# State products of three batch pairs kept in DRAM, w_in in its own column order, the score operand loaded in one piece of 128 rows, and a new hand-written order

## The chip, the cores and the metric

One core of one Trainium2 chip runs the whole program. The metric is device microseconds of one execution. All values in and out are float32; the matmul operands are rounded pieces of float32 ("hi" and "lo"), so that three matmuls (hi·hi, hi·lo, lo·hi) stand for one product.

## What is computed

`x` is [8, 8, 512, 64] (batch, heads, tokens, depth), `state` is [8, 8, 32, 64]. Each head attends both ways, and the 512 token reads and 32 state reads of a batch are then rows of a feed-forward layer:

```python
scores = scale * x @ state.T          # softmax over the 32 states -> a
xread  = a @ state
scores2 = scale * state @ x.T         # softmax over the 512 tokens -> a2
sread  = a2 @ x
rows = concat([xread, sread])         # 8 * 544 = 4352 rows of 512
h = rows @ w_in                       # 512 x 1024
solu = h * softmax(h)
ln = (solu - mean) / sqrt(var + 1e-6) * g_ln
out = ln @ w_out                      # 1024 x 512
```

`w_in` and `w_out` come as 64-bit floats and are turned into float32 on the chip from their two 32-bit words.

## The kernel before, in words

**Fold.** `xread @ w_in` is `a @ (state @ w_in)`. For each pair of batches k (0 to 3) the products state·w_in are made first (`state_w_in`, step V{k}{c}{n}: row block c of w_in, column half n; three matmuls into one PSUM bank at line 277, then two copies of 64 rows each, line 282, into the tiles `swf` of the two batches). `split_state_w_in` (step P) rounds `swf` to `swh` and keeps the rest as `swl`. The 32 token tiles of 128 rows (t = 0 to 31, four per batch) then multiply the softmax matrix with these (`h_steps`, step H, line 447: 12 matmuls). The two last tiles, t = 32 and 33, hold the state reads of all batches and multiply with `whi`/`wlo` themselves.

**A batch.** `load_x` (steps LT) brings the transposed x as two tiles `xT` of 128 partitions, each by two loads of 64 partitions (line 170); `load_xn` (Ln) brings x by tokens; `score` (S, line 319) makes all scores in two PSUM banks; `softmax_tokens` (E) and `softmax_states` (A) make both softmaxes, E with a round trip through DRAM (`e2d`); `read_tokens` (R, line 400) makes the state reads.

**A tile.** After H the chain C (lines 454 to 477: maximum, exponential, product, centring, square sum, scale); then the bounce D (lines 483 to 488: a transpose of 32x32 blocks on VectorE, a store `ut` to DRAM and a load `back` that rearranges it); then T (lines 491 to 502: `uh` and `ul`, rounded part and rest); then O (line 514: 24 matmuls with `wohi`, `wolo`), a scaled copy `osb` and a store: line 527 for token tiles, lines 530 and 531 for the tiles of state reads. There the DRAM side is `b r d` with four batches outermost, while the SBUF side has 128 rows.

**Weights.** `load_w` (l0 to l7 w_in, l8 to l15 w_out, 512 KB each), `low_words` (cl, ScalarE, line 193), `to_f32` (c, VectorE and GpSimd, lines 204 to 210), `split_w_in` (wi: `whi` on ScalarE, `wlo` on VectorE, both written through `placed`, line 216, a strided view that puts the 1024 columns in the order in which the bounce wants them), `split_w_out` (wo: `wohi`, `wolo`, with -g folded in).

**Order.** `ORDER` is a list written out in the file; `issue` walks it and takes one yield of the named step at each word (`*n`: n of them). Every engine has one queue, worked strictly in that order; all loads and stores are issued by SyncE (SP), and a step that waits holds up whatever follows on its engine. `OPT` gives, by letters (a ScalarE, d VectorE, p GpSimd), the engine of each copy, subtraction and so on. The step K is a matmul of the identity with itself, put where TensorE would be idle. The tiles share 43 blocks of 4 KB a partition (`k4`). PSUM has four banks for `ps_t` and four for two h tiles.

The order before begins:

```
K l0 Lg l1 l2 l3 l4 l5 LT000 LT001 LT010 c0 cl0 l6 c0 l7 l8 c0 l9 cl1 c1 l10 c1 l11 LT011 c1 Ls0 cl2 Ls1 Lg c2 l12
wi0 c2 l13 l14 c3 l15 c2 c3 Ln00 cl3 Ln01 Ln10 cl4 Ln11 wi0 c3 cl5 c4 wi1 c4 c5 c4 c5 wi1 c5 cl6 c6 wi2 c6 c7*2 cl7
wi2 cl8 c7 c8 cl9 c8*2 c9 wo0 c10*2 cl10 c9 c10 Q0 G0 c9 cl11 c6 wo1 c11 K*60 S0 LT100 LT101 LT110 LT111 G1 c11 wi3
wo1 A0 c11 cl12 A0 wo2 A0 Q0 wo3 Q1 wi3 K*14 V000 Ls2 A0 cl13 cl14 c12 V000 V001 c12 V000 Q1 V001 A0 V010 wo0 Ls3
c12 V010 A0 V001 cl15 V011 A0 wo4 V010 A0 E0 V011 V020 wo4 P00 E0 A0 V011 P00 E0 V021 wo2 A0 V030*2 E0 H0 A0 H0
V030 V021 H1 V020 wo3 V031 V021 H1 V031 c13 V100 E0 Q2 c14 H0 V031 E0 H1 c14 V101 V020 Q2 c14 V110 P01 V101 V111
V100 P10 H0 c15 H1 c15 P01 P11 E0*2 V101 H0 c15 V100 V110 E0 H0 V111 c13 H1 P20 H1 P11 C0 V110 S1 LT200 LT201 C1
V111 E0 C0 G2 E1 C1 C0 E1 c13 C1 H2 C0 H2 R0 C0 D0 R0 Ln20 Ln21 H3 wo5 C0 R0 D0 H3 A1 E1 R0 wo5 H3 wo6 R0 H3 E1 H3
```

Of the kernel before, what the change touches and what calls it, by code (L numbers as in the profile page):

```python
# [8 lines left out]
F32 = mybir.dt.float32  # L9
# [9 lines left out]
P = 128  # L19
# [9 lines left out]
OPT = dict(ph=2, k4=43, nat=[], s2='p', add='ddpdppdddddppppp', whi='aaaa', wlo='dddd', spl='ppdp',  # L29
           ev='aadaadaaaadaaaaddadadaaaaaadddddaaaaaadadaaaaaadaddadaaaadaadada', swh='aaaaaaaddaddddad',  # L30
           swl='pppppdpppppppdpd', sub='pppppppp', mul='ppdddppd', ath='adaddada', alo='ppdppppd',
           up='aaadadaaadadadaaadaddddaadadaadaaa',
           uh='adaaaddaaadadaddaaadddadddaadaadaddadaddaaaadadaaaaaaaadadaadddaaaad',
           ul='dpdpppppddppppppddpddpdpdpppddpppdppdppppdppppddddddpdpppddpppppdddd',
           oe='aaddaaddaadadadaddadaaddaaaadddaaa')

ORDER = """
K l0 Lg l1 l2 l3 l4 l5 LT000 LT001 LT010 c0 cl0 l6 c0 l7 l8 c0 l9 cl1 c1 l10 c1 l11 LT011 c1 Ls0 cl2 Ls1 Lg c2 l12
wi0 c2 l13 l14 c3 l15 c2 c3 Ln00 cl3 Ln01 Ln10 cl4 Ln11 wi0 c3 cl5 c4 wi1 c4 c5 c4 c5 wi1 c5 cl6 c6 wi2 c6 c7*2 cl7
wi2 cl8 c7 c8 cl9 c8*2 c9 wo0 c10*2 cl10 c9 c10 Q0 G0 c9 cl11 c6 wo1 c11 K*60 S0 LT100 LT101 LT110 LT111 G1 c11 wi3  # L40
wo1 A0 c11 cl12 A0 wo2 A0 Q0 wo3 Q1 wi3 K*14 V000 Ls2 A0 cl13 cl14 c12 V000 V001 c12 V000 Q1 V001 A0 V010 wo0 Ls3
c12 V010 A0 V001 cl15 V011 A0 wo4 V010 A0 E0 V011 V020 wo4 P00 E0 A0 V011 P00 E0 V021 wo2 A0 V030*2 E0 H0 A0 H0
# [15 lines left out]
D10 C11 O8*2 T8 D11 V221 O8 C11 O8 T8 O8 V221 T8 O8 T9 O8*2 T9 T10 O8 T10 O8*3 D11 T10 T9 T10 O9 T9 O8 O9*2 O8 O9*4
T11 O9*2 T11 O9 T11 O9 T11 O9 H13 O9 H13*2 O9 H13 V230 R2 V230 V231 R3 R2 V230 R2 R3 H12 V231 R3*2 S4 P40 P41 V231
C12 O10*3 E4 C12 O10 C13 E4 O10*2 C12 O10 C13 O10*2 C12 H14 C13 H14*2 C12 C13 H14*2 D12 C13 H14 C12 H15 D13 D12 H15  # L60
E4 H15 C13 H15 E4 D13 H15 LT500 P50 LT501 H15 E4*2 P41 LT510 O10 A4 LT511 O10 D12 A4 O10 A4 O11 D13 O11*2 P50 E4*2
O11*3 O10 E4 O11 P51 S5 LT600 LT601 A4 O10 C14 O11*2 E5 O11 LT610 LT611 C14 O11 P51 T12 O11 T12 A4 O12*3 T12 T13
# [40 lines left out]
def attention_then_solu_ffn(ctx, tc, xT, xn, stB, w_in, w_out, g, out):  # L103
# [515 lines left out]
```

## Time and profile before

| what | us |
|---|---|
| median of 3 runs (417.55 to 417.89) | 417.82 |
| profiled execution: its own time | 420.33 |
| its span, first to last instruction | 418.6 |
| PE busy in the span | 369.9 |
| VectorE (DVE) busy | 332.9 |
| ScalarE (ACT) busy | 221.6 |
| GpSimd (POOL) busy | 198.5 |

The transfers that SP issues move 79.18 MB and take 59.6% of 16 DMA engines' span.

How to read it: busy time counts the instructions of an engine, not its waits. PE's is the union of overlapping, pipelined matmuls, so that the mean duration of a matmul in a row (about 0.39 us for 512 columns) is more than the distance from one to the next. The groups of instructions give mean durations by line and tile name; the DMA view gives transfers with the median from issue to landing; the stretches of time give each engine's busy time, the DMA engines' busy share (mean over 16, 1.00 is all of them) and GB/s between two times. Times in all of them are microseconds from the span's start.

### The profile page before, as it was taken

How to read it: one execution, taken by the hardware profiler on the slowest of the kernel's cores; microseconds unless marked ns; L12 is line 12 of the kernel's file. 1: busy time of each engine (PE TensorE's matmuls, PEld its weight loads, DVE VectorE, ACT ScalarE, POOL GpSimd, SP SyncE). 2: the span in 40 equal slices, each digit the busy share in tenths (PEclk: the TensorE clock that was granted, in tenths of full speed). 3: DMA queues.
4: the chain of work that ended last, by engine and by line, in shares of the span. 5: the costliest groups of instructions: out<-in, count | busy, mean ns of one | idle time of the engine just before them, and what ended most of it. 6: DMA issues, size and time to landing. Idle time of an engine off the chain costs nothing.

```text
span 418.6 us, 6204 instructions
## 1 busy us (share of the span) xinstructions
PE 369.9 (88%) x2222; PEld 285.6 (68%) x2222; DVE 332.9 (80%) x436; ACT 221.6 (53%) x347; POOL 198.5 (47%) x257
## 2 busy tenths in 40 slices
PE   8606593887999989999989999989999999999995
PEld 8603362665876768886667676768768688788875
DVE  2898999898998998848989898886899957653631
ACT  2647686666536644827257364534537636624631
POOL 0206787586741746234864448636553214423300
PEclk9955799799999989999999999999999999999998
DMA  7999804776377586950898848545214385352361
GB/s 221 229 313 365 172 8 133 246 225 227 109 249 221 178 276 201 302 176 27 223 294 283 297 161 224 188 148 194 108 69 144 109 290 203 115 198 82 145 201 50
DMA packets 43194, 79.57 MB, mean 190 GB/s; under 512 B 3100, under 2 KB 24860, under 8 KB 43164
## 3 DMA queue, kind: packets, MB, share of 16 engines
q1 hardware_dynamic: 43164, 79.18, 59.6%
q8 instruction: 17, 0.28, 0.3%
q14 instruction: 13, 0.11, 0.1%
HBM read 48.24 MB, written 30.93 MB: 189 GB/s over the span
## 4 chain that ended last, share of the span: by engine, by line
PE 32%; DVE 30%; DMA 23%; issue 6%; ACT 4%; POOL 3%; SPq 2%; DVEq 0%; POOLq 0%; ACTq 0%
PE o L514 17%; PE h L447 11%; DMA back<-ut 7%; DMA ut<-ub 6%; DMA xT<-xT_dram 5%; DVE u L460 4%; DVE ub L483 3%; DVE sm L454 3%; DMA st<-stB_dram 3%; DVE wolo L236 2%; DVE wf L207 2%; DVE z L368 2%; PE swps L277 2%; DVE swf L134 2%; DVE ul L137 2%
## 5 line engine op out<-in xcount | busy, mean ns | idle before, releaser
L137 POOL TENSOR_TENSOR ul<-back,uh 128x512 fp32r<-128x512 f32 x40 | 54.5, 1366 | 59.4 <-DVE uh L134 34.7
L514 PE MATMUL o<-wohi,uh 128*128 128x512 f32 (+1 forms) x280 | 76.4, 394 | 6.8 <-DVE uh L134 3.1
L514 PE MATMUL o<-wolo,uh 128*128 128x512 f32 (+1 forms) x280 | 75.9, 389 | 0.1
L514 PE MATMUL o<-wohi,ul 128*128 128x512 f32 (+1 forms) x280 | 74.4, 384 | 0.0
L514 PEld LDWEIGHTS o<-wohi,uh 128*128 128x128 f32 x280 | 50.6, 189 | 22.9 <-ACT uh L132 5.3
L457 ACT ACTIVATE e<-h,sm 128x1024 f32<-128x1024 f32 x34 | 37.8, 1113 | 52.0 <-DVE sm L454 50.1
L514 PEld LDWEIGHTS o<-wolo,uh 128*128 128x128 f32 x280 | 52.0, 190 | 12.1 <-issue 0.8
L514 PEld LDWEIGHTS o<-wohi,ul 128*128 128x128 f32 x280 | 51.7, 188 | 11.2 <-issue 0.8
L454 DVE TENSOR_REDUCE sm<-h 128x1 f32<-128x1024 f32 x34 | 41.2, 1215 | 15.4 <-PE h L447 9.3
L460 DVE SCALAR_TENSOR_TENSOR u<-h,e 128x1024 f32<-128x1024 f32 x34 | 41.3, 1217 | 10.0 <-ACT e L457 9.4
L447 PE MATMUL h<-swh,ath 128*128 128x512 f32 x128 | 41.0, 406 | 8.3 <-DVE u L460 7.8
L472 ACT ACTIVATE e<-u 128x1024 f32<-128x1024 f32 x34 | 36.0, 1058 | 20.5 <-DVE u L467 20.0
L483 DVE STREAM_TRANSPOSE ub<-u 128x1024 f32<-128x1024 f32 x34 | 41.7, 1233 | 4.5 <-ACT u L465 4.0
L447 PE MATMUL h<-swl,ath 128*128 128x512 f32 x128 | 40.6, 399 | 1.8 <-POOL swl L137 1.7
L447 PE MATMUL h<-swh,atl 128*128 128x512 f32 x128 | 39.5, 394 | 0.2 <-POOL atl L137 0.2
L132 ACT ACTIVATE uh<-back 128x512 fp32r<-128x512 f32 x40 | 24.7, 625 | 27.0 <-DMA back<-ut 25.6
L137 DVE TENSOR_TENSOR ul<-back,uh 128x512 fp32r<-128x512 f32 x28 | 22.3, 798 | 17.1 <-ACT uh L132 16.6
L137 POOL TENSOR_TENSOR swl<-swf,swh 128x1024 fp32r<-128x1024 f32 x13 | 33.5, 2582 | 2.5 <-ACT swh L132 1.6
L447 PEld LDWEIGHTS h<-swh,ath 128*128 128x128 f32 x128 | 23.0, 190 | 16.9 <-issue 10.2
L476 POOL TENSOR_TENSOR sm<-sm 128x1 f32<-128x1 f32 x34 | 8.4, 248 | 50.1 <-ACT e L472 49.1
L132 ACT ACTIVATE swf<-swps 64x512 f32<-64x512 f32 x43 | 24.7, 589 | 12.2 <-PE swps L277 7.4
L319 PE MATMUL sps<-xT,s 64*32 64x512 f32 x128 | 13.9, 658 | 19.0 <-POOL s L134 17.3
(83 smaller groups left out, 625.4 us busy)
## 6 DMA issues: line engine op xcount, KB each, us to landing
ut<-ub SPq DMA_DIRECT2D x34, 512.0 KB, 3.0
back<-ut SPq DMA_DIRECT2D x34, 512.0 KB, 4.5
out_dram<-osb SPq DMA_DIRECT2D x33, 256.0 KB, 3.6
xT<-xT_dram SPq DMA_DIRECT2D x32, 256.0 KB, 7.1
xn<-xn_dram SPq DMA_DIRECT2D x16, 512.0 KB, 6.5
raw<-w_in_dram SPq DMA_DIRECT2D x8, 512.0 KB, 11.4
raw<-w_out_dram SPq DMA_DIRECT2D x8, 512.0 KB, 12.0
e2d<-e2b SPq DMA_DIRECT2D x8, 512.0 KB, 4.4
```

The costliest lines, as they stand in the source:

```text
L132: nc.scalar.activation(out, src, AF.Copy)
L134: engine(k).tensor_copy(out, src)
L137: engine(k).tensor_tensor(out=out, in0=a, in1=hi.bitcast(F32), op=ALU.subtract)
L319: nc.tensor.matmul(ps[j][at:at + NS, :], s2[b // 2][rows, c, (b % 2) ^ c, k, :], x_of[b, k][rows, c, :], start=True, stop=True)
L447: nc.tensor.matmul(ph[t][:, cols], left[l][:, p, tok], right[r][:, cols], start=(p, l, r) == (0, 0, 0), stop=(p, l, r) == (parts - 1, *kin ...
L454: nc.vector.tensor_reduce(nm, ph[t], AX.X, ALU.max, negate=True)
L457: nc.scalar.activation(e, ph[t], AF.Exp, bias=nm, accum_out=z)
L460: nc.vector.scalar_tensor_tensor(out=u, in0=ph[t], scalar=1.0, in1=e, op0=ALU.mult, op1=ALU.mult, accum_out=su)
L472: nc.scalar.activation(e, u, AF.Square, scale=float(DF) ** -0.5, accum_out=ss)
L476: nc.gpsimd.tensor_tensor(out=t1, in0=t1, in1=ss, op=ALU.add)
L483: nc.vector.transpose(ub, us[t][0])
L514: nc.tensor.matmul(po, ut[t][l][:, f, :], w[NP + f // 2][:, f % 2, cols], start=(hf, l, w is wohi, q) == (0, 0, True, 0), stop=(hf, l, q) ...
```

## The change

- Only pair 0 (`direct=[0]`) is still copied from PSUM straight into `swf`. For pairs 1 to 3 one copy of all 128 rows goes into a tile `vt`, a store (step Y, four per pair, 512 KB) keeps it in DRAM, and a load (step Z, one per `swf` tile, 512 KB) brings back the rows of one batch. All matmuls of V stand ahead of the first of O.
- The column order moves: `whi` and `wlo` are written straight; the loads of w_out take its rows in the permuted order instead; `gT` is loaded by four transfers with a strided destination (two elements a partition each). `wlo` is made on GpSimd.
- `load_x` is one transfer of 128 rows: the destination is 128 partitions, the source is `r d (c s)` with r = 2 outermost. The 32 LT steps become 16.
- `load_st` brings two pairs at once, into `k4` blocks; the operands `sp` are `k4` blocks; `k4` is 45; the head swap of odd batches goes.
- OPT and ORDER are new.

```diff
-OPT = dict(ph=2, k4=43, nat=[], s2='p', add='ddpdppdddddppppp', whi='aaaa', wlo='dddd', spl='ppdp',
+OPT = dict(ph=2, k4=45, s2='p', add='ddpddpppdpdppppd', whi='aaaa', wlo='pppp', spl='pdpd',
...
+K l0 l1 Lg Ls0 c0 cl0 c0 Ls2 l2 c0 cl1 l3 Lg c1 l4 c1 l5 c1 l6 Q0 G0 LT00 Q1 LT01 wi0 Q1 G1 LT10 Q2 c2 LT11 G2 c2
+cl2 Q3 c3 LT20 Q2 c3 cl3 cl4 LT21 G3 c4*2 l7 c5 Q0 c5 l8 c2 c4 l9 cl5 wi0 c3 cl6 K*60 S0 l10 l11 E0 K*2 V000 c5 wi1
+A0 l12 A0 V000 E0 wi1 A0 E0 l13 wi2 K*8 V001 E0 c6 l14 V001 E0 c6 V001 A0 l15 c7 E0 K*7 V010 cl7 V011 Ln00 V010 E0
+wi2 E0 A0 Ln01 c7 V011 V010 E0 c6 cl8 K*12 V020 A0 P00 LT30 A0 c7 V020 A0 LT31 cl9 P00 A0 wi3 A0 cl10 wi3 V020 K*21
+H0 H1 V000 V021 Q3 H1 H0 A0 V021 V030 V021 V030 V011 K*2 V031 V030 c8 E0 V100 V031 c8 V101 P01 c8 H1 V031 H0 V101
+P01 c9 H1 cl11 H0 V100 S1 wo0 Y10 V110 c9 P10 H1 E1 c9 H1 V110 wo0 H0 P11 H0 E1 V111 C0 E1 V111 E1 C0 c10 K*6 R0
+Y11 E1 c10 R0 P10 c10 E1 wo1 V120 cl12 E1 P11 E1 V120 cl13 V121 C0 E1 wo2 V121 wo1 H2 C0 Y12 V130 R0 wo2 R0 C1 C0
+H2 E1 H2*2 D0 V130 C0 H2 C1 V131 R0*2 D0 c11 H2 c11 V131 V200 C1 c11 Y13 V201 V200 V201 A1 H3 cl14 H3 Y20 A1 V210
+D0 wo3 A1 V211 C1 wo3 H3 A1 V220 V211 C1 V221 V210 V230 D1 V220 Y21 C1 V231 V221 Ln10 c12 V230 H3 D1 c13 V300 V231
+c13 V301 T0 c12 c13 V300 C2 V310 Y22 V301 V311 c12 T0 V310 H3 Ln11 V311 V320 cl15 V321 c14 D1 c15 V320 H3 c15 V330
+V321 Y23 c15 T0 V331 Y30 C3 V330 T0 Z20 O0 R1 A1 c14 Z21 R1 Ln20 Ln21 C2 O0 A1 c14 O0*2 T1 A1 O0 C2 V331 O0 T1 O1
+wo4 O1 C2 wo5 O1 A1 Y31 O1 D2 T1 O1 wo6 O1 wo5 O1 D2 C2 T1 O0 A1 wo7 C2 A1 C3 O1 O0 A1 H4*2 wo6 H4*2 wo4 H4 Y32 wo7
...
+H7 C5 P30 O4*2 D5 O4*2 A2 D5 H7 T4 H7 C6 H7*2 Z40 A2 O4 T4 C6 O4 R2 D5 R2 Ln30 C6 Ln31 O4 T4 O4*2 O3 C6 O4 R2 C5 O3
+C7 O4 C6 LT40 O4 LT41 H8 D6 H8 C7 C6 H8 O4 H8 D6 H8 T5 P31 H8 P40 C7 O5*3 O4 C8 C7 H9*2 T5 H9 C8 H9 D7 H9 C7 H9 C8
+O5 D7 O5 T5 C7 D6 O5 C8 O5 D8 O5 C8 O5*2 T5 P40 D7 R2 D8 H10 R2*2 O5*2 C8 S3 O5 T6 C9 O5 H10 P31 H10 O6 E3 C9 O6 A3
+O6*2 A3 T7 E3 H10 T6 A3 E3 H10 D8 H10 O7 E3 T6 O6 T7 E3 O6 E3 T6 O6*2 A3 T7 O6*2 E3 A3 O6 T7 O6 C9 O7 T8 O7 O6 O8
+T8 H11 O6 A3 T8 H11*2 T8 H11 A3 H11 E3 H11 A3 O8 C10 O8 E3 O8 LT50 O8 C9 C10 O8*2 D9 O8 C9 O8 E3 A3 O8 D9 O8 C9
+LT51 O8 A3 O7 O8 C10 O7 A3 O7*2 C11 H12*2 C10 R3 C11 H12 D10 H12 D9 C10 H12*2 C11 D10 R3 C10 LT60 O7 Ln40 C11 O7
+Ln41 D11 O7 C11 O7*2 Z41 R3 D11 C11 H13 T9 O7 R3 O9 R3 O7 R3 O9 C12 T9 D10 O9*2 C12 H13 T9 O9 T9 O9 C12 O9*3 C12
+H14 D12 H14 C12 H14*2 P41 D12 C12 H14*2 D11 O9 O8 P41 O9*2 H13 O9 H13*3 T10 S4 T10 C13 O10 D12 E4 O10 C13 O10 T10
+E4 A4 O10 T10 E4 O10 C13 O10 T11 O10 E4 H15 O9 C13 T11 A4 H15*2 A4 C13 H15 E4 H15 D13 H15 A4 E4 O10 T11 O10 E4 D13
+O10 E4 Z50 O10 A4 C13 LT61 O10 T12 E4 O11 O10 O12 LT70 T12 A4 O12 O10 O12 D13 O12 A4 T12 T11 O12 A4 O12 P50 O12*2
+T12 O12 A4 O12*2 E4 C14 O12 A4 O11*2 P50 O12 O11*2 C14 O11 C15 O11*2 A4 C15 O11*3 C14 T13 O11 S5 O11 T13 C14 C15
+O11 H16*3 T13 E5 H16 D14 C14 H16 E5 H16 O12 H17 T13 E5 C14 D14 H17 C16 H17*3 E5 C16 H17 C15 E5 R4 D15 D14 E5 R4
...
+LT71 D17 O15 H19 C17 Z51 H19 C18 H19 Z60 T16 O14 Z61 O14 Z70 T16 C18 O14 O16*2 T16 C18 O16 D17 O14 O16 T16 O16 C18
+O14 H20 C19 H20 C18 H20 D18 O16*2 C19 C18 O16 P51 D18 O16 P51 O16 H20 O16 C19 H20*2 P60 O16 C19 H21 P60 H21 C19 H21
+T17 H21 O15 T17 H21 C19 D19 H21 T17 D18 O17*2 O16 T17 D19 O17 P61 O17 O16 O17*2 C20 O17*2 P70 O17 C20 O17 P61 P70
...
+    kept = ctx.enter_context(tc.tile_pool(name="kept", bufs=4, space=bass.MemoryType.DRAM))
...
-        nc.sync.dma_start(gT, g)
+        for c in range(NFC // 2):
+            nc.sync.dma_start(gT.rearrange("x (a c) -> x c a", a=2)[:, c],
+                              g[c * NS:(c + 1) * NS].rearrange("f (p a) -> (f p) a", p=4))
...
-    def load_x(b, k, r):
-        if (b, k) not in x_of:
-            x_of[b, k] = block([2, S], F32, f"xT{b}_{k}")
-        src = xT[b].rearrange("(k d) (r c) s -> k r d c s", k=2, r=2)
-        nc.sync.dma_start(x_of[b, k][r * D:(r + 1) * D], src[k, r])
+    def load_x(b, k):
+        x_of[b, k] = block([2, S], F32, f"xT{b}_{k}")
+        nc.sync.dma_start(x_of[b, k].rearrange("p c s -> p (c s)"),
+                          xT[b].rearrange("(k d) (r c) s -> k r d (c s)", k=2, r=2)[k])
...
+            src = w_out.bitcast(U32).rearrange("(p c f) h -> c f p h", p=4, f=NS)[n - 2 * NP]
+            nc.sync.dma_start(raw[n].rearrange("p h k -> p (h k)"), src)
...
-        copy(of("whi", c), placed(whi[c]), src)
+        copy(of("whi", c), whi[c], src)
-        minus(of("wlo", c), placed(wlo[c]), src, placed(whi[c]))
+        minus(of("wlo", c), wlo[c], src, whi[c])
...
+        if k not in OPT["direct"]:
+            copy(of("ev", 16 * k + 4 * c + 2 * n), vt[k, c][:, cols], ps)
+            yield
+            return
...
+    def keep_state_w_in(k, c):
+        if k not in kd:
+            kd[k] = kept.tile([NP * P * DF], F32, tag="kept", name=f"kept{k}")
+        nc.sync.dma_start(kd[k].rearrange("(c p f) -> c p f", c=NP, p=P)[c], vt[k, c])
+        yield
+
+    def load_state_w_in(b, j):
+        swf[b, j] = block([DF], F32, f"swf{b}_{j}")
+        halves = kd[b // 2].rearrange("(j a p f) -> j a p f", j=NJ, a=4, p=D)[j]
+        nc.sync.dma_start(swf[b, j], halves[1:3] if b % 2 else halves[0::3])
+        yield
```

More of the change, by code (lines that the diff above doesn't have):

```diff
@@ L37 @@
-ORDER = """
[L38 to L42, printed above, removed]
@@ L58 @@
[L58 to L62, printed above, removed]
@@ L268, in state_w_in @@
         cols = slice(n * HALF, (n + 1) * HALF)
[L269 to L273 removed]
+        if k in OPT["direct"]:
+            for b in (2 * k, 2 * k + 1):
+                if (b, j) not in swf:
+                    swf[b, j] = block([DF], F32, f"swf{b}_{j}")
+        elif n == 0:
+            vt[k, c] = block([DF], F32, f"vt{k}_{c}")
         ps = bank([HALF], f"swps{k}_{c}_{n}")
@@ L567, in attention_then_solu_ffn @@
         step(f"R{b}", read_tokens, b)
-        for j in range(NJ if b not in OPT["nat"] else 0):
+        for j in range(NJ):
+            step(f"Z{b}{j}", load_state_w_in, b, j)
             step(f"P{b}{j}", split_state_w_in, b, j)
```

131 lines of the change are left out of this document (53 added, 78 removed).

## The prediction

> **What bounds the kernel now.** I read the page first, for the totals.
>
> ```profile
> PE 369.9 (88%) x2222; PEld 285.6 (68%) x2222; DVE 332.9 (80%) x436; ACT 221.6 (53%) x347; POOL 198.5 (47%) x257
> ...
> DMA packets 43194, 79.57 MB, mean 190 GB/s; under 512 B 3100, under 2 KB 24860, under 8 KB 43164
> ```
>
> No engine fills the span, so I went to the stretches of time, cut where the character of the work changes, and for the load side where the kind of load changes.
>
> ```profile
> core 0 of [0], span 418.6 us
> core 0: us, PE busy (x) PEld busy (x) DVE busy (x) ACT busy (x) POOL busy (x), PEclk, DMA share, GB/s
> 2.00:12.00 10.00, 10.00 (x72) 10.00 (x72) 4.40 (x9) 2.32 (x5) 0.00 (x0) 1.00 0.93 291
> 12.00:22.00 10.00, 5.66 (x51) 5.47 (x49) 8.77 (x10) 5.57 (x5) 3.87 (x3) 0.91 1.05 197
> 36.00:42.00 6.00, 6.00 (x39) 4.05 (x38) 4.35 (x5) 5.56 (x8) 5.24 (x9) 0.62 1.05 387
> 55.70:86.60 30.90, 22.90 (x164) 16.25 (x164) 29.00 (x40) 23.21 (x39) 21.23 (x21) 0.89 0.50 157
> 86.60:113.00 26.40, 23.25 (x172) 16.94 (x173) 24.99 (x35) 15.93 (x25) 19.22 (x25) 1.00 0.51 173
> 350.00:375.00 25.00, 25.00 (x116) 20.23 (x115) 16.06 (x21) 13.17 (x22) 9.74 (x16) 1.00 0.46 159
> 412.00:414.00 2.00, 1.69 (x15) 1.49 (x13) 0.00 (x0) 0.27 (x1) 0.00 (x0) 1.00 0.26 100
> ```
>
> Up to 42 us the loads are the limit (share about 1). From 56 to 113 it is VectorE: 29.00 of 30.90 and 24.99 of 26.40 us, 94%, with PE short of work. Late it is PE, 25.00 of 25.00. The timeline shows what ends each stage.
>
> ```profile
> 5.50 2.31 SPq L170 DMA_DIRECT2D xT<-xT_dram  x3
> ...
> 9.20 2.17 SPq L184 DMA_DIRECT2D raw<-w_in_dram  x2
> ...
> 23.85 0.67 ACT L193 ACTIVATE r<-raw 128x512 uint32<-128x512 uint32 x1 [2.93 <-DMA raw<-w_in_dram]
> ...
> 44.77 1.06 ACT L365 ACTIVATE a<-a 128x1024 f32<-128x1024 f32 x1
> ```
>
> The load l6, issued at 9.20 behind three xT loads, is only used at 23.85: transfers are served in the order of their issue. The exponential of A0 starts at 44.77. On PE alone:
>
> ```profile
> 34.97 3.45 PE L319 MATMUL sps<-xT,s 64*32 64x512 f32 x16 [17.31 <-POOL s L134]
> ...
> 55.69 0.74 PE L447 MATMUL h<-swh,ath 128*128 128x512 f32 x2 [0.38 <-ACT ath L132]
> ...
> 113.03 1.07 PE L447 MATMUL h<-swh,ath 128*128 128x512 f32 x4
> ```
>
> The first scores start at 34.97, the first h tile 20.7 us later. At 113.03 H5 starts; by then the order has issued 180 of its 1344 large matmuls (H, O and V, 512 columns), so the other 1164 take 418.6 - 113.0 = 305.6 us, 0.2625 us each with all gaps.
>
> **The change where it saves.** These are the durations it trades, of the tile `swf` (ns, minimum, median, maximum) and of the two halves of w_in.
>
> ```profile
> L132 ACT ACTIVATE swf<-swps x43: 572/592/595, 43.5 to 301.6; 64x512 f32<-64x512 f32 x43
> L134 DVE COPY swf<-swps x21: 620/684/695, 46.6 to 300.0; 64x512 f32<-64x512 f32 x21
> L137 POOL TENSOR_TENSOR swl<-swf,swh x13: 2347/2398/3271, 53.4 to 301.8; 128x1024 fp32r<-128x1024 f32 x13
> L132 ACT ACTIVATE swh<-swf x9: 1041/1057/1062, 50.5 to 300.6; 128x1024 fp32r<-128x1024 f32 x9
> ```
>
> ```profile
> L137 DVE TENSOR_TENSOR wlo<-wf,whi 128x1024 fp32r<-128x1024 f32 x4 | 8.6, 2143 | 0.9 <-ACT whi L132 0.9
> ...
> L132 ACT ACTIVATE whi<-wf 128x1024 fp32r<-128x1024 f32 x4 | 8.2, 2053 | 0.0
> ```
>
> Copies out of PSUM: 64 half ones cost 43 x 0.592 + 21 x 0.684 = 39.8 us. Now 16 stay halves (10 ScalarE, 6 VectorE: 10.0) and 24 are whole (22 ScalarE, 2 VectorE). No whole copy of this kind is in the trace; it has the same 512 columns, so I bound it by 0.592 and twice that and take the upper median, 0.684: 16.4. That saves 13.4 us on two engines. `whi` written straight should cost what the straight `swh` costs, 4 x (2.053 - 1.057) = 4.0 us off ScalarE. `wlo` leaves VectorE (8.6 us) for GpSimd (4 x 2.4 = 9.6 us on an engine busy 198.5 of 418.6). The other new letters shift a few operations between the engines. The head swap, fewer state loads and the longer k4 cost nothing: no instruction is added, and the loads carry the same bytes. The 88 more K matmuls stand where PE waits for VectorE and the loads; without that cover they are 88 x 10.0/72 (the first stretch is all K) = 12 us. `gT` has 1024 short runs instead of 128 rows: between 0 and, at the 2 KB packet time that the 100 GB/s of four engines below makes (82 ns), 64 per engine x 0.082 = 5.2 us ahead of the other loads; I take 1, since the runs are tiny. Twelve stores Y and twelve loads Z of 512 KB add 12.6 MB to 79.57; at 387 GB/s 33 us of transfers in a span whose queue is 60% busy. SP meets the Y's between E and D stores, and a late copy there would hold up the bounce behind it; the copies follow their matmuls within a step or two, so I take 0 (bound: one copy each, 12 x 0.684 = 8 us).
>
> With every transfer on all 16 engines the new order would then win. Ahead of the first LT stand nine 512 KB loads, 4.72 MB at 291 GB/s: 2 + 16.2 + 1 = 19 us. LT00 and LT01 take 1.05 MB at 387 GB/s, 2.7: scores at 22, the first h tile 20.7 later, at 43. Adding the mean durations of the VectorE steps between two places of the new order gives 38.5 us from there to the first O, 41 at 94%; by then 144 large matmuls are out instead of 96, and 180 after another 11 us of VectorE, 12 at 94%: at 96, where the old order has them at 113. The rest is 1164 x 0.2625, plus 3 for VectorE, which has about 264 us left in it instead of 250. Span: 418.6 - 17 + 3 = 405.
>
> **The change where it costs.** The new xT load has 128 rows in SBUF, but its source is r d (c s): the outermost dimension is 2. A source that can't be read as 128 even rows also belongs to the Z loads of even batches, `halves[0::3]`; `halves[1:3]` is one contiguous piece. Before, only the three stores of the state-read tiles (lines 530, 531) have such a side, with 4 outermost.
>
> ```profile
> 408.44 6.33 SPq L531 DMA_DIRECT2D out_dram<-osb  x3
> ...
> 411.49 3.27 SPq L531 DMA_DIRECT2D out_dram<-osb  x2
> ...
> DMA packets 251, 0.34 MB, mean 85 GB/s; under 512 B 8, under 2 KB 163, under 8 KB 251
> ...
> ut<-ub SPq DMA_DIRECT2D x34, 512.0 KB, 3.0
> back<-ut SPq DMA_DIRECT2D x34, 512.0 KB, 4.5
> ```
>
> They run at a share of 0.26 and 100 GB/s (412 to 414 above), against 1.05 and 387 for loads of 128 even rows: four engines of 16 at 25 GB/s each. The small packets say the same: 3100 for the 188 issues of the DMA view, 16 each, but 8 for the two landings between 412 and 416 (the third row), four each. And the second store, issued at 411.49 while the first was under way, opens no other engines: the share stays 0.26. So with 2 outermost I expect two engines, the same two each time: 524 KB / 50 GB/s = 10.5 us a load, and every later transfer has its share on those two engines behind it. The trace shows 4 and not 2, and a store and not a load; the bounds for one load are 1.4 us (16 engines) and 10.5, and I take 10.5.
>
> The Trainium skill, "DMA: Bandwidth & Descriptors", section "Why a DMA increments its semaphore by 16 and not by 1", says that a transfer uses the largest number up to 16 that divides the slowest dimension of both sides. By that rule the new xT loads get two engines; the stores' rows agree with it at four.
>
> *Start.* LT00 to LT21 are six such loads in a row: 19 + 6 x 10.5 = 82 us, l7 lands at 83.3. In the new order the first step of c7 stands on VectorE ahead of the rest of A0 and E0, and cl7 on ScalarE ahead of A0's exponential. In the old kernel that exponential starts at 44.77 and the first h tile 10.9 us later, with weight work between; I take 8. First h tile at 91 instead of 43: 48 us lost.
>
> *Later groups*, each loss = loads x 10.5 + landing (4.5 if only the read is behind them, 3.0 + 4.5 if the store is too) - the time to the first user, in large matmuls of the order x 0.2625:
> - LT30, LT31 at the start of H0: they begin behind l8 to l15, Ln00, Ln01 and the E0 store (11 x 1.4 after 83.3, so 99), end at 120, E0's read is there at 121; R0 stands 11.3 us of VectorE behind H0, 12 at 94%, and would come at 103: 18.
> - Z20, Z21 ahead of D2; T2 is 20.5 us of VectorE on, 21.8 at 94%: 21 + 7.5 - 21.8 = 7.
> - Z40, LT40, LT41 ahead of D6's store; 66 matmuls to T6, 17.3: 31.5 + 7.5 - 17.3 = 22.
> - LT50, LT51 ahead of D9's read; 48 to T9, 12.6: 21 + 4.5 - 12.6 = 13. LT60, Z41 right after, till 42; T10 at 94 matmuls + 13 = 37.7: 46.5 - 37.7 = 9. LT61, LT70 ahead of D13's read; 48 to T13: 13.
> - LT71, Z60, Z61 ahead of D17's read; 54 to T17, 14.2: 31.5 + 4.5 - 14.2 = 22.
>
> Together 104. Behind T17 no such load is left, and 582 large matmuls go at PE's own pace, since VectorE has caught up: between 25.00/116 = 0.216 us (the stretch at 350, PE never idle) and 0.2625, I take 0.24, so 582 x 0.0225 = 13 less. Span: 405 + 48 + 104 - 13 = 544; the weakest factor is the 10.5, where longer packets may gain a little, and I say 541. What is late next once these loads are in the way is the bounce (T waits for `back`), not VectorE.
>
> The profiled execution took 420.33 us, 1.7 beyond its span, and the median of the runs, 417.82, is 0.8 under the span: predicted 540.
>
> **Rivals.** *All 16 engines after all* (chance 0.09): the xT pattern is split by its 128 SBUF rows, and the change does what its words say. For it: no load of this shape is in the trace. Against it: the stores have 128 SBUF rows too. Span 405, time 404, faster; it decides from 16 engines down to about 8, where the six first loads (16 us) no longer hold l7 up. The Trainium skill, "SBUF — State Buffer", section on the DMA port swizzle, speaks for this case: 64 rows reach only half the ports, and one transfer should span all 128. The rows at 12 to 22 (64-row loads, 197 GB/s at share 1.05) agree with its half; its rule would give the 404.
> *Slow at the start only* (0.12): two engines, but the later groups hide, as the loads stand 40 to 100 matmuls ahead of their own users and the tiles in flight cover the bounce. Against it: T follows D's store by 10 to 14 us, less than any group. Span 405 + 48 = 453, time 452.
> *Nothing overlaps*: the 16 later slow loads cost 10.5 each, 168: span 608 with the 13 off. I give it no chance of its own, it is the far bound.
>
> **How the numbers follow.** Main case 0.79, 540 (own range 480 to 590); start only 0.12; 16 engines 0.09. The range 455 to 590 leaves out the fast case, half of the start-only case's lower side and the main case's tails, together about 0.2. 0.2% of this time, 0.8 us, is about what a measurement can tell: faster 0.09, within it 0.01 (a start-only case that gains later), slower 0.90.
>
> **What would show it.** Right: xT rows with a median to landing of 10 us or more; a DMA share near 0.13 and 50 GB/s between 25 and 80 us, no c7 ahead of 80, the first h tile near 91; ScalarE and GpSimd waiting for `back` behind Z and LT. Wrong: scores at 22 and a h tile at 43 with a DMA share of 1 between. `whi` should show 1.06 us and the whole copies 0.68 in either case.

## The result, and the profile after

The changed kernel took 578.09 us (median of 4 runs, 575.78 to 578.91) against 417.69 us for the kernel before (412.98 to 417.89, 4 runs): 1.387 times as long, interval 1.376 to 1.398. Its profiled execution took 577.46 us, span 575.7. The page, its engines and its transfers:

```profile
PE 392.9 (68%) x2310; PEld 309.0 (54%) x2310; DVE 321.0 (56%) x425; ACT 211.2 (37%) x342; POOL 190.2 (33%) x249
...
DMA packets 46744, 92.18 MB, mean 160 GB/s; under 512 B 3832, under 2 KB 25592, under 8 KB 46712
```

VectorE has 12 us less work than before (321.0 against 332.9) and no engine is near its span, so all of them wait more. PE's sum grew by 23 us: there are 88 more K matmuls, and the granted clock is lower (0.84 in the mean, 0.95 before; 0.50 in some of the stretches below). The stretches of time show where it begins (columns as in the prediction; the last two are the DMA share and GB/s):

```profile
20.00:40.00 20.00, 5.03 (x21) 1.66 (x22) 1.09 (x2) 2.16 (x3) 5.10 (x6) 0.50 0.13 52
40.00:60.00 20.00, 9.07 (x66) 8.13 (x65) 5.42 (x6) 4.17 (x8) 8.45 (x5) 0.84 0.13 52
60.00:80.00 20.00, 0.00 (x0) 0.00 (x0) 0.00 (x0) 0.00 (x0) 0.00 (x0) 0.50 0.71 201
```

Where the kernel before moved 387 GB/s at a share of 1.05 (36 to 42 us), this one moves 52 at 0.13: two engines of 16 (0.13 x 16 = 2.1), at 26 GB/s each. From 60 to 80 us nothing computes at all, while the even loads that stood behind those of two pieces come in. The timeline, in order of time:

```profile
8.39 45.48 SPq L173 DMA_DIRECT2D xT<-xT_dram  x6
...
26.82 1.92 PE L339 MATMUL sps<-xT,s 64*32 64x512 f32 x4 [9.33 <-DMA xT<-xT_dram]
36.89 1.95 PE L339 MATMUL sps<-xT,s 64*32 64x512 f32 x12 [8.15 <-DMA xT<-xT_dram]
53.91 9.93 SPq L190 DMA_DIRECT2D raw<-w_in_dram  x1
63.89 20.19 SPq L193 DMA_DIRECT2D raw<-w_out_dram  x8
83.55 0.67 ACT L202 ACTIVATE r<-raw 128x512 uint32<-128x512 uint32 x1 [38.17 <-DMA raw<-w_in_dram]
94.59 1.19 PE L463 MATMUL h<-swh,ath 128*128 128x512 f32 x4
121.20 1.93 PE L416 MATMUL srps<-xn,e 128*32 128x64 f32 x64 [13.00 <-issue]
```

The scores of the first two halves start 10.07 us apart: one slow load each. The six issues alone hold SP for 45.48 us, l7 is first used at 83.55 after ScalarE stood 38.17 us, and the first h tile comes at 94.59 instead of 55.69. Later it is the bounce. The waits of the changed kernel (us in total, times, longest), and then the same row of the kernel before:

```profile
ACT uh L132 <- DMA back<-ut: 74.2, 13, 18.7
...
DVE swh L134 <- DMA swf<-kept: 33.2, 3, 18.3
```

```profile
ACT uh L132 <- DMA back<-ut: 25.6, 12, 5.3
```

Single waits grow from 5.3 to 18.7 us, about two slow loads. The saving did come; these rows of tiles answer to the prediction's of `swf` and `swh` (ns, minimum, median, maximum):

```profile
L132 ACT ACTIVATE vt<-swps x22: 577/598/605, 101.0 to 152.6; 128x512 f32<-128x512 f32 x22
...
L134 DVE COPY vt<-swps x2: 674/676/678, 137.8 to 138.4; 128x512 f32<-128x512 f32 x2
...
L132 ACT ACTIVATE whi<-wf x4: 1041/1046/1054, 9.9 to 89.9; 128x1024 fp32r<-128x1024 f32 x4
...
L137 POOL TENSOR_TENSOR wlo<-wf,whi x4: 2357/2592/2806, 21.2 to 91.3; 128x1024 fp32r<-128x1024 f32 x4
```

A copy of 128 rows out of PSUM (598 and 676 ns) costs what a copy of 64 rows costs (592 and 684 in the prediction's rows).

### The profile page after: what moved, and what is told of

Same layout as the page of the kernel before. It is cut to its first block, busy times and chain, and to the rows that moved or that the text cites. A ratio compares the mean times of both kernels' runs of the same rounds, so it can differ in the third digit from the quotient of the medians.

```text
span 575.7 us, 6359 instructions
## 1 busy us (share of the span) xinstructions
PE 392.9 (68%) x2310; PEld 309.0 (54%) x2310; DVE 321.0 (56%) x425; ACT 211.2 (37%) x342; POOL 190.2 (33%) x249
## 4 chain that ended last, share of the span: by engine, by line
DMA 33%; PE 33%; SPq 12%; DVE 11%; issue 5%; ACT 3%; POOL 2%; ACTq 0%; DVEq 0%; POOLq 0%
PE o L531 19%; DMA back<-ut 14%; DMA ut<-ub 9%; PE h L463 9%; SPq L173 8%; DMA raw<-w_in_dram 6%; DMA swf<-kept 2%; SPq L180 2%; PE swps L282 2%; DMA xn<-xn_dram 2%; DVE u L476 1%; DVE ub L500 1%; PE warm L555 1%; PE srps L416 1%; DVE u L483 1%
## 5 line engine op out<-in xcount | busy, mean ns | idle before, releaser
L531 PE MATMUL o<-wohi,uh 128*128 128x512 f32 (+1 forms) x280 | 81.4, 413 | 63.3 <-DVE uh L134 38.8
L531 PEld LDWEIGHTS o<-wohi,uh 128*128 128x128 f32 x280 | 53.6, 201 | 80.3 <-ACT uh L132 27.6
L137 POOL TENSOR_TENSOR ul<-back,uh 128x512 fp32r<-128x512 f32 x32 | 44.0, 1376 | 72.6 <-ACT uh L132 41.9
L463 PE MATMUL h<-swh,ath 128*128 128x512 f32 x128 | 44.0, 430 | 33.8 <-DVE u L476 27.9
L132 ACT ACTIVATE uh<-back 128x512 fp32r<-128x512 f32 x48 | 29.7, 622 | 83.7 <-DMA back<-ut 74.2
L531 PEld LDWEIGHTS o<-wohi,ul 128*128 128x128 f32 x280 | 52.6, 192 | 11.9 <-DVE ul L137 0.6
L282 PE MATMUL swps<-whi,sp 128*128 128x512 f32 x64 | 26.5, 444 | 39.1 <-ACT swf L132 38.1
L137 DVE TENSOR_TENSOR ul<-back,uh 128x512 fp32r<-128x512 f32 x36 | 28.1, 785 | 40.3 <-ACT uh L132 40.1
L137 POOL TENSOR_TENSOR swl<-swf,swh 128x1024 fp32r<-128x1024 f32 x11 | 27.8, 2535 | 66.0 <-DVE swh L134 41.5
L488 ACT ACTIVATE e<-u 128x1024 f32<-128x1024 f32 x34 | 35.9, 1055 | 14.6 <-DVE u L483 14.2
L481 ACT ACTIVATE u<-u,sm 128x1024 f32<-128x1024 f32 x22 | 25.2, 1147 | 40.4 <-DVE u L476 40.4
L282 PEld LDWEIGHTS swps<-whi,sp 128*128 128x128 f32 x64 | 13.2, 206 | 44.7 <-ACT swf L132 38.3
```

The lines of the kernel that those rows point to most:

```text
L132: nc.scalar.activation(out, src, AF.Copy)
L137: engine(k).tensor_tensor(out=out, in0=a, in1=hi.bitcast(F32), op=ALU.subtract)
L282: nc.tensor.matmul(ps, l[:, c], r[:, cols], start=x == 0, stop=x == 2)
L463: nc.tensor.matmul(ph[t][:, cols], left[l][:, p, tok], right[r][:, cols], start=(p, l, r) == (0, 0, 0), stop=(p, l, r) == (parts - 1, *kin ...
L481: nc.scalar.activation(u, u, AF.Identity, bias=su, scale=-float(DF))
L488: nc.scalar.activation(e, u, AF.Square, scale=float(DF) ** -0.5, accum_out=ss)
```

## The experiments

The theory: a transfer whose DRAM side is not one even sequence of rows runs on as many DMA engines as it has outermost pieces, 2 here, and whatever is behind it waits. Rivals: the start alone costs, the later groups hide; the price lies in the new order, which bunches the loads; the price lies in the queue they are issued on. A result with one run is a single time beside single or repeated runs of the kernel before on the same chip. The runs e1 to e4 were on one chip and e5 to e12 on another; the kernel before took 417.35 us on the first (7 runs) and 418.64 on the second (17 runs; the single 420.48 below is another one).

**e1: both kinds of load as two halves of 64 rows.**

```diff
-        nc.sync.dma_start(x_of[b, k].rearrange("p c s -> p (c s)"),
-                          xT[b].rearrange("(k d) (r c) s -> k r d (c s)", k=2, r=2)[k])
+        whole = x_of[b, k].rearrange("p c s -> p (c s)")
+        src = xT[b].rearrange("(k d) (r c) s -> k r d (c s)", k=2, r=2)[k]
+        for r in range(2):
+            nc.sync.dma_start(whole[r * D:(r + 1) * D], src[r])
...
-        nc.sync.dma_start(swf[b, j], halves[1:3] if b % 2 else halves[0::3])
+        if b % 2:
+            nc.sync.dma_start(swf[b, j], halves[1:3])
+        else:
+            for q in range(2):
+                nc.sync.dma_start(swf[b, j][q * D:(q + 1) * D], halves[3 * q])
```

> The new kernel with only the transfers undone whose source has 2 outermost: each xT load and each swf load of an even batch goes out as two loads of 64 rows. Theory (two engines for such a source): all of the loss goes, the median is 407 us (400 to 415), first h tile near 45 us, faster than the kernel before. Rival (the new order, or the 12.6 MB through DRAM with 24 more transfers on SP's queue, costs most of it): 480 us or more.

Measured: 407.76 us (406.62 to 409.12), ratio 0.979 [0.974, 0.984], span 404.8. The whole loss is gone with the two patterns. Its timeline:

```profile
19.85 5.29 PE L345 MATMUL sps<-xT,s 64*32 64x512 f32 x16 [1.92 <-DMA xT<-xT_dram]
45.14 2.04 PE L469 MATMUL h<-swh,ath 128*128 128x512 f32 x4 [2.69 <-DVE ath L134]
```

**e2 and e3: one of the two alone.** In e2 only the xT loads are halved and the Z loads keep two pieces; in e3 the other way round (the two halves of the diff above).

> The new kernel with only the xT loads split in two; the six swf loads of even batches stay one transfer with 2 outermost. Theory: xT carries most of the loss; the swf loads leave Z20 and Z21 (7 us), Z40 (1) and Z60 and Z61 (12): about 427 us, between 410 and 445. If the swf loads matter as much each as the xT loads: 575 - 16/22 x 170 = 450.

> The new kernel with only the swf loads of even batches split; the 16 xT loads stay one transfer with 2 outermost. Theory: start 48 us and the xT part of the later groups stay: 500 to 550 us, the stretch from 20 to 60 us again at share 0.13 and 52 GB/s. Rival (the swf loads are the main cost): below 460.

Measured: 459.41 us with slow Z loads alone (span 457.6), 527.19 with slow xT loads alone (span 525.4), one run each. Over e1's span that is 52.8 and 120.6 us, together 173.4; the change as it is shows 575.7 - 404.8 = 170.9. The two kinds add up. e2 missed its range (410 to 445): a slow Z load costs 52.8 / 6 = 8.8 us, nearly its whole length, and the expectation's other case, a Z load as dear as an xT load (450), is the nearer one.

**e4: the same single load of 128 rows, from an even source.** The host lays xT out so that each half is 128 rows in sequence; Z as in e1.

```diff
-                          xT[b].rearrange("(k d) (r c) s -> k r d (c s)", k=2, r=2)[k])
+                          xT[b, k])
...
-        "xT": c(x.reshape(B, NP, 2, S, D).transpose(0, 2, 4, 1, 3)).reshape(B, P, NP, S),
+        "xT": c(x.reshape(B, 2, 2, 2, S, D).transpose(0, 3, 1, 5, 2, 4)).reshape(B, 2, P, 2 * S),
```

> The swf loads split as in the first run, and the host lays xT out so that the 128 rows of one xT load follow each other: one transfer of 128 even rows, all 16 engines. Theory: 1.36 us of transfer in place of 2.66 for each, the six loads ahead of l7 cost 8 us less: first h tile near 40 us, median 402 us (396 to 410). Rival (64-row loads are as good as 128): the same as the first run within 0.3%.

Measured: 402.77 us (400.97 to 403.68), ratio 0.965 [0.960, 0.970]. So neither 128 rows in SBUF nor a single transfer is the trouble; the DRAM side is. Here it is one unbroken piece; the next two runs keep gaps in it and change only the number of pieces.

**e5 and e6: 4 and 8 pieces.**

```diff
-        nc.sync.dma_start(x_of[b, k].rearrange("p c s -> p (c s)"),
-                          xT[b].rearrange("(k d) (r c) s -> k r d (c s)", k=2, r=2)[k])
+        nc.sync.dma_start(x_of[b, k].rearrange("p c s -> p (c s)"), xT[b, k][:, :P // 4])
...
+    def spaced(a):
+        wide = np.zeros((B, 2, 4, P // 4 + 1, 2 * S), a.dtype)
+        wide[:, :, :, :P // 4] = a.reshape(B, 2, 4, P // 4, 2 * S)
+        return wide
```

> The changed kernel, but the host lays each half of xT out in DRAM as 4 pieces with a gap of one row between them, so that the source of the one 128-row load is 4 outermost by 32 rows, and the Z loads of even batches are two 64-row loads as in e1. Same bytes, same SBUF side, same order; only the number of outermost pieces of the xT source differs from e3 (2) and e4 (128). Theory (as many DMA engines as the outermost dimension has pieces, 25 GB/s each): 100 GB/s, 5.2 us a load; six first loads 31 us against 63 in e3 and 9 in e4. Over e4 that is 22 us at the start, and the pairs later (10.5 us) hide behind 12 us and more of matmuls: 420 to 435 us, DMA share near 0.26 while they run. Rival (any source that is not one even sequence of rows falls back to one slow path, whatever its number of pieces): as e3, 515 to 540 us, share 0.13.

> As the one before, with 8 pieces of 16 rows. Theory: 200 GB/s, 2.6 us a load, as much as two 64-row loads take in e1, and nothing later is held up: 403 to 411 us, share near 0.5. Rival (one slow path): 515 to 540 us. The prediction named 8 engines as the point from which the change is faster than before; this run tries that point.

Measured, one run each: 456.85 us with 4 pieces, 429.67 with 8, beside 420.48 before. Four stretches, of e5, twice of e6, and of e4, inside their first loads:

```profile
22.00:32.00 10.00, 5.82 (x23) 2.27 (x24) 1.89 (x3) 2.07 (x3) 4.53 (x4) 0.50 0.26 103
```

```profile
16.50:18.00 1.50, 0.50 (x5) 0.30 (x3) 0.23 (x2) 0.00 (x0) 1.34 (x4) 1.00 0.62 115
24.00:30.00 6.00, 2.54 (x15) 0.88 (x16) 1.76 (x2) 1.30 (x2) 0.67 (x1) 0.50 1.05 178
```

```profile
18.00:38.00 20.00, 17.45 (x133) 14.39 (x131) 16.83 (x18) 13.28 (x21) 17.83 (x13) 1.00 1.03 406
```

Share 0.13, 0.26, and 52, 103 GB/s for 2 and 4 pieces: the number of pieces sets the number of engines, and the rival of one slow path falls. The small packets on the pages of e3 (2 pieces), e5 (4), e6 (8) and e4 (128 rows) say the same, for 8 pieces too:

```profile
DMA packets 46923, 92.17 MB, mean 175 GB/s; under 512 B 4012, under 2 KB 25772, under 8 KB 46892
DMA packets 46955, 92.17 MB, mean 203 GB/s; under 512 B 4044, under 2 KB 25804, under 8 KB 46924
DMA packets 47020, 92.17 MB, mean 215 GB/s; under 512 B 4109, under 2 KB 25869, under 8 KB 46989
DMA packets 47147, 92.17 MB, mean 231 GB/s; under 512 B 4236, under 2 KB 25996, under 8 KB 47116
```

Those under 512 B grow by 32, 65 and 127. With one of them for each engine of a load, as the prediction read the stores, 16 loads on 2, 4, 8 and 16 engines give 16 x 2, 16 x 4 and 16 x 8.

But both times are above the expected ranges, by 22 and 19 us. Against e4's 402.8 us, 8 pieces cost 27 us more, 4 cost 54, 2 (e3) cost 124. Four engines lengthen a load by 5.1 - 1.3 = 3.8 us, two by 10.1 - 1.3 = 8.8 (512 KB at 103, 52 and 406 GB/s): 54 / 3.8 and 124 / 8.8 are both 14 of the 16 loads. Hardly any of it hides. With 8 pieces the engines themselves are slower: from 16.5 to 18 us, before l7 is issued at 17.95, the xT loads move 115 GB/s, 14 an engine where 2 and 4 pieces give 26, and a load takes 4.6 us, not the 2.6 expected. Of these longer loads about half hides: 27 / (4.6 - 1.3) = 8 of 16. Why eight engines are slower each stays open. Later, with the loads behind them under way too (24 to 30 us), all engines are counted busy at 178 GB/s.

**e7: the merged load alone, in the kernel before and its own order.**

```diff
-        if (b, k) not in x_of:
-            x_of[b, k] = block([2, S], F32, f"xT{b}_{k}")
-        src = xT[b].rearrange("(k d) (r c) s -> k r d c s", k=2, r=2)
-        nc.sync.dma_start(x_of[b, k][r * D:(r + 1) * D], src[k, r])
+        if (b, k) in x_of:
+            return
+        x_of[b, k] = block([2, S], F32, f"xT{b}_{k}")
+        nc.sync.dma_start(x_of[b, k].rearrange("p c s -> p (c s)"),
+                          xT[b].rearrange("(k d) (r c) s -> k r d (c s)", k=2, r=2)[k])
```

> The kernel before with one part of the change alone: its two 64-row loads of an xT half become the one 128-row load whose source has 2 pieces (it is issued at the place of the first of the two). Nothing else differs. Theory (two engines, 10.5 us a load, later transfers behind them): LT00 and LT01 hold l6 up by 21 - 5 = 16 us; the pairs later stand 21 us long ahead of reads of `back` that are wanted within some 13 us, about 10 us each with the landing, 7 pairs: 16 + 70 less what hides, 455 to 510 us. Rival (the loads cost only because the new order bunches them): 418 to 430 us.

Measured: 540.54 us, one run, beside 420.48: this one edit costs the old order 120 us, as much as it costs the new one (e3, 120.6), and more than expected (455 to 510 in all). The rival that blames the bunching falls. Its wait for the bounce looks like the changed kernel's:

```profile
ACT uh L132 <- DMA back<-ut: 94.1, 19, 17.9
```

**e8: the loads of two pieces on ScalarE's queue.**

```diff
-        nc.sync.dma_start(x_of[b, k].rearrange("p c s -> p (c s)"),
+        nc.scalar.dma_start(x_of[b, k].rearrange("p c s -> p (c s)"),
...
-        nc.sync.dma_start(swf[b, j], halves[1:3] if b % 2 else halves[0::3])
+        queue = nc.sync if b % 2 else nc.scalar
+        queue.dma_start(swf[b, j], halves[1:3] if b % 2 else halves[0::3])
```

> The changed kernel with the loads that have 2 pieces (all xT, and the Z loads of even batches) issued from ScalarE's queue instead of SP's; the rest of the order and all shapes stay. Theory A (what costs is the first-in first-out of SP's queue on the two engines, and SP itself being held until its earlier transfers land): l7 to l15 and the bounces no longer stand behind the slow loads and share the two engines with them instead; most of the 170 us goes, 420 to 470 us. Theory B (what costs is that the two engines move 50 GB/s, whoever issued the transfer): each slow load is still 10.5 us of those two engines, and every transfer has its share on them: 510 to 575 us.

Measured: 574.94 us, one run, at the upper end of what theory B named; theory A's 420 to 470 is refuted. The trace makes it a weaker proof of B. On ScalarE's timeline the issue itself stands:

```profile
10.86 15.58 ACTq L173 DMA_DIRECT2D xT<-xT_dram  x1
...
26.51 11.95 ACTq L173 DMA_DIRECT2D xT<-xT_dram  x1
...
38.56 11.91 ACTq L173 DMA_DIRECT2D xT<-xT_dram  x1
```

From the third load on, an issue takes as long as a slow load or longer, and ScalarE's own work stands behind it. SP isn't free either; among its waits:

```profile
SPq L193 <- DMA xT<-xT_dram: 67.4, 6, 11.7
```

By the profile, SP's w_out loads l8 and on wait six times for the landing of an xT load that they don't need. So this run doesn't separate a slow pair of engines from the hold that slow loads put on whoever issues.

**e9: the first six slow, the ten later ones halved.**

```diff
-        for r in range(2):
-            nc.sync.dma_start(whole[r * D:(r + 1) * D], src[r])
+        if b < 3:
+            nc.sync.dma_start(whole, src)
+        else:
+            for r in range(2):
+                nc.sync.dma_start(whole[r * D:(r + 1) * D], src[r])
```

> As e1 (every load with 2 pieces issued as two 64-row loads), but the six xT loads that the new order bunches at the start (LT00 to LT21) keep their 2 pieces and two engines; the ten later ones stay halved. It tells the start from the later groups. The prediction's sum for the start: 48 us over the fast start, so 408 + 48 = 456 (450 to 462), and 525 - 456 = 70 us of e3 then belong to the ten later xT loads. Rival 1 (slow at the start only, the later groups hide): close to e3, 515 to 527. Rival 2 (the six loads cost more than their own time, because the even loads l8 to l15 behind them also run at 165 to 236 GB/s instead of 390 until 84 us): 465 to 480.

Measured: 451.25 us, one run. The start costs 451.25 - 407.76 = 43 us, the ten later xT loads 527.19 - 451.25 = 76, the Z loads some 52. Both rivals fall: the later groups don't hide, and the start costs no more than its own loads (six of them, each 7.9 us longer than its two halves, as worked out below, make 47).

**e10: the even load alone, in the kernel before** (the edit of e4 in the old `load_x`).

> The kernel before, in its own order, with one edit: the host lays the xT halves out so that each half is one load of 128 even rows instead of two 64-row loads. It asks how much of e4's 15 us gain is the load and how much the new order. The 64-row pairs take 2.66 us per 512 KB at 197 GB/s, the even load 1.3; the two first pairs hold up the load-bound start by 2.7 us, a further pair by 1.3. Theory (the order is what gains): 413 to 417 us, ratio 0.99 to 1.00. Rival (the load alone gains as much as e4): 403 to 406.

Measured: 416.11 us (414.11 to 418.31) against 418.64, ratio 0.994 [0.992, 0.997]: 2.5 us. In the old order the even load alone is worth 0.6%. In the new order the same load is worth more, 5.0 us or 1.2% (e1 407.76, e4 402.77), and the 2.1% that e1 has without it are the work taken off the engines and the new order.

**e11: the loads of two pieces from GpSimd's queue** (the diff of e8 with `nc.gpsimd`).

> The changed kernel with its loads of 2 pieces (all xT, Z of even batches) issued from GpSimd's queue. It asks whether two pieces always mean the same two engines. If the two engines are the same for each transfer as they were from SP and ScalarE: 52 GB/s in the stretch of the six first loads, 550 to 600 us as before. If each transfer takes two engines, but other ones in turn: several loads run side by side, 150 GB/s or more in that stretch, and the time falls to 430 to 500 us; GpSimd, busy 190 us of the span, would pay for each issue with some of its time.

Measured: 491.77 us, one run, 86 less than the change as it is. The queues (packets, MB, share of 16 engines; q0 is GpSimd's, q1 SP's) from 20 to 40 us, then from 45 to 55, and the page's packets:

```profile
q1 hardware_dynamic: 1348, 4.17, 75.5%
q0 software_dynamic: 3101, 0.89, 34.9%
```

```profile
q0 software_dynamic: 2119, 1.50, 67.4%
q1 hardware_dynamic: 131, 0.29, 12.2%
```

```profile
DMA packets 66763, 92.25 MB, mean 188 GB/s; under 512 B 23852, under 2 KB 45612, under 8 KB 66732
```

Until 40 us SP's even loads fill the engines, and the loads of two pieces get no more than 0.89 MB in 20 us through, 44 GB/s. Once SP's are done (45 to 55 us), they move 1.50 MB in 10 us, 150 GB/s at a share of 0.67, where SP's queue gave 52 at 0.13; so from this queue the transfers don't all take the same two engines. The Trainium skill, "DMA: Bandwidth & Descriptors", section "Why a DMA increments its semaphore by 16 and not by 1", says that SP's and ScalarE's transfers take the lowest-numbered engines and GpSimd's take neighbouring ones from a cursor that moves on. The two traces agree with it in these shares; which engines by number they were, they don't show. A single load still takes long (a median of 18.6 us to landing for xT), and there are 20,000 more small packets.

**e12: e4 with g in one load, and the state-read tiles in even stores.**

```diff
-        for c in range(NFC // 2):
-            nc.sync.dma_start(gT.rearrange("x (a c) -> x c a", a=2)[:, c],
-                              g[c * NS:(c + 1) * NS].rearrange("f (p a) -> (f p) a", p=4))
+        nc.sync.dma_start(gT, g)
...
-                rows = out.rearrange("(b r) d -> b r d", r=ROWS)[b:b + P // NS, S:, cols]
-                nc.sync.dma_start(rows, o[:, cols])
+                for q in range(P // NS):
+                    row = (b + q) * ROWS + S
+                    queue = nc.sync if q % 2 else nc.scalar
+                    queue.dma_start(out[row:row + NS, cols], o[q * NS:(q + 1) * NS, cols])
...
-        "g": c(moe_g_ln.reshape(NFC, P).T),
+        "g": c(moe_g_ln.reshape(NFC, P).T.reshape(4, NS, 4, 2).transpose(1, 2, 3, 0)).reshape(P, NFC),
```

> e4 (one load of 128 even rows for each xT half, Z of even batches as two 64-row loads) with two more loads and stores made even: the host lays out g so that gT is one load of 128 rows instead of four loads of 4-byte runs, which frees SP for some 2 us of its first 4.3 us; and the stores of the state-read tiles (4 pieces, 100 GB/s) go as four stores of 32 even rows each, on SP's and ScalarE's queues in turn, which takes 1 to 3 us off the last 10 us. Expected 398 to 401 us against 403 for e4; if the start hides the g loads and the end is set by PE and one landing, 402 to 403.

Measured: 398.80 us (396.91 to 401.85) against 418.64, ratio 0.955 [0.951, 0.959], the best of all. The last matmuls and the spans, of e4 and then of e12:

```profile
span 399.2 us, 6372 instructions
...
393.52 0.64 PE L534 MATMUL o<-wohi,ul 128*128 128x256 f32 x4
```

```profile
span 397.2 us, 6378 instructions
...
393.11 0.64 PE L531 MATMUL o<-wohi,ul 128*128 128x256 f32 x4
```

Behind the last matmul e4 still takes 399.2 - 394.2 = 5.0 us, e12 397.2 - 393.8 = 3.4. So 1.6 of the 2.0 us between these two spans come from the stores; of the two microseconds of g loads freed at the start 0.4 are left at the last matmul. These are single executions; the medians lie 4.0 us apart, on two chips.

## Why the prediction was right, and where it was not

Forecast 540 us (455 to 590), measured 578: the mechanism was right and the size 38 us short, inside the range and inside the main case's own range.

*The saving and the fast kernel.* Copies and `whi` came as worked out: 24 whole copies took 22 x 0.598 + 2 x 0.676 = 14.5 us, not 16.4, and `whi` 1.046. `wlo` took 10.3 us on GpSimd, not 9.6. The span of 405 for 16 engines is e1's 404.8, with scores at 19.85 (22 forecast) and the first h tile at 45.14 (43). The g loads, put at 1 us, cost some 0.4 (e12).

*Two engines, 10.5 us a load, fixed.* Right: 52 GB/s at 0.13, scores 10.07 us apart. The share was forecast up to 80 us; it ended by 60, as the even loads behind then ran too. The landing times that the prediction named as a sign aren't in this trace. The bridge from a store with 4 pieces to a load with 2 held; e5 shows the 4.

*The start.* l7 landed at 83.5 (83.3 forecast), the first h tile came at 94.59 (91), 49.5 us behind e1's (48).

*The later groups.* To see each, I counted PE's large matmuls (H, O, V) along the timelines of the changed kernel and of e1, which issue the same ones in the same order, and took the difference of the times at which the nth starts; the steps in it are the groups.

| up to large matmul | delay, us | step | forecast | group | loads x 7.9 |
|---|---|---|---|---|---|
| 20 | 48.6 | 48.6 | 48 | LT00 to LT21 | 47 |
| 70 | 58.2 | 9.6 | 18 | LT30, LT31 | 16 |
| 310 | 74.5 | 16.3 | 7 | Z20, Z21 | 16 |
| 400 | 102.6 | 28.1 | 22 | Z40, LT40, LT41 | 24 |
| 490 | 117.5 | 14.9 | 13 | LT50, LT51 | 16 |
| 540 | 131.7 | 14.2 | 9 | LT60, Z41 | 16 |
| 640 | 147.1 | 15.4 | 13 | LT61, LT70 | 16 |
| 800 | 172.0 | 24.9 | 22 | LT71, Z60, Z61 | 24 |

The steps behind the start sum to 123 us; the forecast was 104. Three groups are within 3 us, LT30/31 is 8 over-priced, and three are under-priced, Z20/21 by 9. The last column fits better than the forecast. In e1 the same loads, as halves, move 234 GB/s, 2.2 us each, so a slow one of 10.1 is 7.9 us longer:

```profile
18.00:30.00 12.00, 10.09 (x43) 5.23 (x44) 5.74 (x9) 4.38 (x7) 10.66 (x10) 0.72 1.05 234
```

All groups but LT30/31 lose this whole extra length, within 5 us, and all 22 loads together make 22 x 7.9 = 174, where the spans differ by 170.9. In the old order e7 agrees: 120 us for 16 loads, 7.5 each. So the mis-sized term is the time to the first user, which I took off for every group: outside LT30/31 it hid next to nothing. What stands behind the loads instead, one place shows. There the step that failed is "ahead of D2; T2 is 20.5 us of VectorE on": I took the bounce as the first user behind the group. The changed kernel's timeline shows another:

```profile
151.70 11.50 SPq L180 DMA_DIRECT2D xn<-xn_dram  x2
...
166.55 0.37 SPq L321 DMA_DIRECT2D ut<-ub  x1
...
179.56 1.23 DVE L476 SCALAR_TENSOR_TENSOR u<-h,e 128x1024 f32<-128x1024 f32 x1 [17.32 <-DMA kept<-vt]
```

Behind Z20 and Z21 stand stores of `vt` too. VectorE stands 17.32 us in front of a chain step for such a store to land, and that step reads nothing of it: as I read it, `u` is written into a `k4` block that `vt` gives back only then. A late store holds its buffer, and with 45 blocks the next writer wants it at once. That the other groups lose theirs in the same way (one wait of GpSimd's `swl` for an `ut` store, 18.7 us, speaks for it) was not tried.

*Thirteen microseconds for a faster pace after T17.* This step failed whole: the delay is 172.0 us at matmul 800 and 170.6 at 1350. The same 645 matmuls, of the changed kernel and of e1:

```profile
444.50:560.60 116.10, 115.36 (x645) 92.91 (x644) 86.05 (x114) 56.31 (x90) 46.47 (x71) 1.00 0.53 180
```

```profile
273.40:390.60 117.20, 115.78 (x645) 92.73 (x644) 86.68 (x117) 57.35 (x91) 46.53 (x71) 1.00 0.51 180
```

PE is the limit in both, so there was no slack to catch up with. The 0.2625 us a matmul that I spread over the whole rest was, in the kernel before, an average of 0.27 ahead of this place and 0.23 behind it. Together the 19 of the groups and the 12 that were not caught up make the shortfall of the span, 575.7 against 544; the 3 taken off for longer packets were not there either, and the median lies 2.4 us above the span where 0.8 below it was taken.

*The rivals.* All 16 engines: refuted, 52 GB/s. Its side remark, that it decides from about 8 engines up, was wrong: at 8 the kernel is 429.67 us against 420.48, so the point lies between 8 and 16. Slow at the start only: refuted by e9. "Nothing overlaps", the far bound given no chance, was the nearer truth as a mechanism. Its 168 us counted 10.5 for each of the 16 later loads, though the fast kernel also spends 2.2 on each; 16 x 7.9 = 126 is what it gives against e1, and 123 are lost.

## What to carry to other kernels

Before merging two loads into one, read the DRAM side as the transfer carries it: 2, 4 and 8 outermost pieces gave these loads 2, 4 and 8 engines, and 128 even rows gave them 16. Let the host or an earlier store lay the data out in even rows; where it can't, two even transfers of 64 rows beat one uneven transfer here, even one of 8 pieces. Price an uneven transfer at its full extra length, not at its length less the slack of its own user: in a tight order like this one something behind it (a store that holds a buffer, the issuing engine, a bounce) wanted the queue nearly every time. When a stretch is lost, check what limits the rest before crediting it with catching up.

## What was unexpected of the hardware

- The issue of a transfer with 2 pieces holds its engine once two or so are under way: 11.9 to 15.6 us for each of the next four on ScalarE, 45.48 us for six on SP, where e4's even ones go out in 6.38 (six issues). Issuing was not free where the engines behind it were few.
- 8 pieces were not twice as good as 4 nor equal to two halves of 64 rows: 115 GB/s for the loads alone, against 103 and 234, and 429.67 us against e1's 407.76.
- From GpSimd's queue the same two-piece loads moved 150 GB/s at a share of 0.67, yet with a median of 18.6 us from issue to landing for an xT load.
